# Turning k to tokens with an ordinary product instead of a full transpose, in an HGRN2 and bilinear-FFN kernel

## The chip, the cores and the metric

The kernel runs on one core of one Trainium2 chip. The metric is the device time of one execution in microseconds (us), the median of several runs; lower is better. Five engines work side by side in a core: TensorE (PE; its weight loads are listed as PEld), VectorE (DVE), ScalarE (ACT), GpSimd (POOL) and SyncE (SP, which issues transfers). TensorE writes only to PSUM, and another engine copies from there to SBUF.

## The reference: what is computed

A gated linear recurrence feeds a bilinear feed-forward layer. There are 4 batches, 8 heads, 768 tokens and 48 channels a head; then 3072 tokens of width 384 go through two matrices of 384 by 1536 and one of 1536 by 384. All data of the recurrence is float32.

```python
f = 1.0 / (1.0 + np.exp(-f_logit))
for t in range(S):
    state = f[:, :, t, :, None] * state + np.einsum('bhd,bhe->bhde', k[:, :, t], v[:, :, t])
    y[:, :, t] = np.einsum('bhd,bhde->bhe', q[:, :, t], state)
...
x = attn_out.transpose(0, 2, 1, 3).reshape(B * S, H * D)
a = x @ w_a
b = x @ w_b
return a * b @ w_out
```

The product `k[:, :, t]` by `v[:, :, t]` sums over tokens. TensorE sums over the partition axis, so k, which is loaded with its channels on the partitions, has to be turned until its tokens lie there.

## The kernel before

The recurrence is worked off in 16 units. A unit is one batch, one half of the tokens (384) and four heads: two heads lie one above the other on the partitions (rows 0 to 47 and 64 to 111; rows 48 to 63 and 112 to 127 hold zeros for k), and two such pairs lie side by side (`n` = 0, 1). The tokens of a unit are cut into three chunks (`c`) of 128, and each of these into two of 64 (`p`). For each unit the kernel scales q and k by cumulated products of f (`front`), forms the scores inside 64 tokens (`scores`), turns k (`turn`), sums up the states (`gains`), and forms the output from the scores and the states (`within`, `across`). The constants are D = 48, R = 64, SUB = 64, C = 128, NC = 3, BLK = 384.

```python
def turn(u, spare=False):
    kf = halves(sets[u % NSET]["k"])
    kT = sb1.tile([128, 2, NC, 128], FP32, tag="kT", name="kT")
    ps = pair(spare)
    for n in range(2):
        for c in range(NC):
            o = n * BLK + c * C
            nc.tensor.transpose(ps[n][:, c * C:c * C + C], kf[:, o:o + C], ident)      # L347
        if spare:
            nc.scalar.copy(kT[:, n].rearrange("s c x -> s (c x)"), ps[n][:, 0:BLK])    # L349
    if not spare:
        nc.scalar.copy(kT.rearrange("s n c x -> s n (c x)"), ps_x[:, :, 0:BLK])        # L351
    live[u]["kT"] = kT
    give_back(ps)

def gains(u):
    ...
    for n in range(2):
        for c in range(NC):
            for p in range(2):
                ...
                for h in range(2):
                    r = slice(SUB * p, SUB * p + SUB)
                    nc.tensor.matmul(                                                  # L367
                        ps_x[R * h:R * h + D, p, (n * NC + c) * D:(n * NC + c) * D + D],
                        lhsT=kT[r, n, c, R * h:R * h + D],
                        rhs=t["v"][r, n, c, h * D:h * D + D], start=True, stop=True)
    ...
```

A unit's turning is six transposes, each with a piece of k of 128 channels by 128 tokens as the loaded weights and the 128-column identity as the streamed operand. The first four units use spare PSUM banks (`spare`) and two copies of 384 columns each; the other twelve use `ps_x` and one copy of 768 columns. `gains` writes `ps_x` too, after the copy has read it. In the twelve later units the steps are laid between pieces of the feed-forward layer (its products are L469 in `up`, L542 in `up_pair`, L610 in `down`):

```python
def slot(u):
    nxt = front(u + 1) if u + 1 < NU else iter(())
    next(nxt, None)
    yield
    if u > 2 * NQ:
        within(u - 1)          # L401
    if u < NU:
        scores(u)              # L319
    next(nxt, None)
    yield
    if u < NU:
        turn(u)                # L347, L351
    if u > 2 * NQ:
        across(u - 1)          # L422, and the copies of L435
    yield
    if u < NU:
        gains(u)               # L367
    yield
    ...
```

At each `yield` a piece of the feed-forward layer may follow, of a dozen or more products, or none, as a table of times (`when`, `begun_early`) sets it.

Of the kernel before, what the change touches and what calls it, by code (L numbers as in the profile page):

```python
# [11 lines left out]
FP32 = mybir.dt.float32  # L12
# [7 lines left out]
C = 128  # L20
FINE = (0, 1, 2, 4, 8, 16)
BLK = 384
# [3 lines left out]
R = 64  # L26
# [52 lines left out]
def by_quotients(ctx, tc, q, k, f_logit, v, moe_w_a, moe_w_b, moe_w_out, out, ident, weights, bad):  # L79
    nc = tc.nc  # L80
    B, H, D, S = q.shape
# [5 lines left out]
    NC = BLK // C  # L87
# [9 lines left out]
    sb1 = ctx.enter_context(tc.tile_pool(name="sb1", bufs=1))  # L97
# [32 lines left out]
    def unit(u):  # L130
        b, r = divmod(u, NH * NQ)
        return (b, *divmod(r, NQ))
# [118 lines left out]
    def halves(x):  # L251
        return x.rearrange("p n s -> p (n s)")
# [36 lines left out]
    ps_x, ps_y = (ps_a.tile([128, 2, 512], FP32, tag=n, name=n) for n in ("ps_x", "ps_y"))  # L289
# [14 lines left out]
    def pair(spare=False):  # L304

        return [ps_f[idle.pop(0)] if spare else ps_x[:, i] for i in range(2)]

    def give_back(ps):
        idle.extend(i for x in ps for i, bank in enumerate(ps_f) if bank is x)
# [29 lines left out]
    def turn(u, spare=False):  # L339

        kf = halves(sets[u % NSET]["k"])
        kT = sb1.tile([128, 2, NC, 128], FP32, tag="kT", name="kT")
        ps = pair(spare)
        for n in range(2):
            for c in range(NC):
                o = n * BLK + c * C
                nc.tensor.transpose(ps[n][:, c * C:c * C + C], kf[:, o:o + C], ident)  # L347
            if spare:
                nc.scalar.copy(kT[:, n].rearrange("s c x -> s (c x)"), ps[n][:, 0:BLK])  # L349
        if not spare:  # L350
            nc.scalar.copy(kT.rearrange("s n c x -> s n (c x)"), ps_x[:, :, 0:BLK])  # L351
        live[u]["kT"] = kT
        give_back(ps)

    def gains(u):

        _, half, _ = unit(u)
        t, kT = sets[u % NSET], live[u]["kT"]
        last = half == NH - 1
# [3 lines that stand above are left out]
                    if last and c == NC - 1 and p == 1:  # L363
                        continue
                    for h in range(2):
                        r = slice(SUB * p, SUB * p + SUB)
                        nc.tensor.matmul(  # L367
                            ps_x[R * h:R * h + D, p, (n * NC + c) * D:(n * NC + c) * D + D],
                            lhsT=kT[r, n, c, R * h:R * h + D],
                            rhs=t["v"][r, n, c, h * D:h * D + D],  # L370
                            start=True,
                            stop=True,
                        )
        st = sb3.tile([128, NJ, 2, D], FP32, tag="st", name="st")
        before = live[u - NQ]["st"][NJ] if half else None
        live[u]["st"] = [before] + [st[:, j] for j in range(NJ - 1 if last else NJ)]
        for j in range(NJ - 1 if last else NJ):
            c, p = divmod(j, 2)
            new = ps_x[:, p, 0:2 * NC * D].rearrange("r (n c d) -> r n c d", n=2, c=NC)[:, :, c]
            if before is None:  # L380
                nc.vector.tensor_copy(st[:, j], new)
            else:
                nc.vector.tensor_tensor(st[:, j], before, new, ALU.add)
            before = st[:, j]
        before = live[u]["st"][-1]
        if not last:

            for n in range(2):
                end = products_of_f[u][:, n, BLK - 1:BLK]
                nc.vector.tensor_scalar(before[:, n], before[:, n], end, math.exp(-MIDDLE), ALU.mult, ALU.mult)  # L390
# [261 lines left out]
# [12 lines that stand above are left out]
            turn(u)  # L664
        if u > 2 * NQ:
            across(u - 1)
# [8 lines that stand above are left out]
# [26 lines left out]
    with tc.manual_schedule():  # L701
# [35 lines left out]
        load_unit(2, "v")  # L737
        next(fronts[1])
        turn(0, True)
        within(0)  # L740
        gains(0)
        load_unit(NSET, "f")
        load_weights()
        next(fronts[2])
        turn(1, True)
        across(0)
        load_weights()
        scores(1, True)
        end(2)
        within(1, True)  # L750
        load_unit(2, "q")
        gains(1)
        across(1)
        load_weights()
# [496 lines left out]
```

## Time and profile before

| What | Value |
|---|---|
| Time, median of 3 runs | 630.34 us (629.26 to 631.24) |
| Span of the profiled run | 628.2 us |
| PE busy | 592.5 us (94%), 5922 products |
| PEld busy | 535.6 us (85%), 5922 weight loads |
| DVE busy | 378.2 us (60%) |
| ACT busy | 221.3 us (35%) |
| POOL busy | 63.0 us (10%) |

The profile's page gives the busy time of each engine, the span in 40 slices, the DMA queues, the chain of work that ended last, and the costliest groups of instructions. A group's line has the source line, the engine, the operation, out<-in by tile names, the shapes and the count; then busy time in us and the mean ns of one; then the idle time of the engine before them and what ended it. The mean of a product includes its way through the array, and the next product starts before it is over, so what a stream of products costs is read from the distance between starts. The timeline lists merged pieces: start in us, length in us, engine, line, operation, tiles, shapes, count, and in brackets the idle time before and what ended it.

### The profile page before, as it was taken

The page shows a single profiled execution, that of the slowest core. Times are in us where ns is not written, and L with a number is a line of the kernel's source. Part 1 is how long each engine was busy: PE and PEld are TensorE (multiplying, and loading weights), DVE is VectorE, ACT ScalarE, POOL GpSimd, SP SyncE. Part 2 cuts the span into 40 slices and gives each one's busy share as a digit, 9 for nine tenths or more (in the row PEclk, how much of TensorE's full clock was granted, in tenths as well). Part 3 has the DMA queues.
Part 4 walks back from the last instruction along what each step waited for, and adds up shares of the span by engine and source line. Part 5 has one row for each costly group of instructions (what it writes and reads, how often), then busy time and mean ns, then how long its engine had stood idle before and what let it go on. Part 6 is the DMA issues. An engine that isn't in the chain of part 4 may idle for free.

```text
span 628.2 us, 13968 instructions
## 1 busy us (share of the span) xinstructions
PE 592.5 (94%) x5922; PEld 535.6 (85%) x5922; DVE 378.2 (60%) x748; ACT 221.3 (35%) x400; POOL 63.0 (10%) x58
## 2 busy tenths in 40 slices
PE   0859899999999999999999999999999999999995
PEld 0626555558998999999999999999999999999995
DVE  6868444797887567646675567647564344534541
ACT  6576498822332243224312242323311232022200
POOL 6243154410000000000000000000000000000000
PEclk9959999999999999999999999999999999999999
DMA  8786785000144404130404012040001000000000
GB/s 237 230 255 175 168 263 197 1 1 1 41 109 114 100 3 94 33 91 1 96 1 120 27 36 62 12 110 2 20 1 46 26 20 2 2 27 0 1 26 30
DMA packets 30343, 43.65 MB, mean 69 GB/s; under 512 B 3776, under 2 KB 24896, under 8 KB 30272
## 3 DMA queue, kind: packets, MB, share of 16 engines
q1 hardware_dynamic: 29984, 42.38, 25.0%
q8 instruction: 48, 0.79, 0.5%
q10 hardware_dynamic: 288, 0.30, 0.2%
q14 instruction: 23, 0.19, 0.1%
HBM read 33.23 MB, written 4.72 MB: 60 GB/s over the span
## 4 chain that ended last, share of the span: by engine, by line
PE 88%; DMA 4%; DVE 2%; ACT 2%; SPq 2%; issue 1%; ACTq 0%; DVEq 0%
PE ps_f L542 41%; PE ps_f L610 23%; PE ps_f L469 14%; DMA xT<-y 2%; PE ps_y L401 2%; PE ps_y L422 2%; PE ps_x L319 2%; PE ps_x L367 2%; PE ps_x L347 1%; SPq L154 1%; DMA raw<-in_moe_w_b_dram 1%; SPq L450 1%; DMA out_dram<-o 1%; ACT y L435 1%; DVE h L605 0%
## 5 line engine op out<-in xcount | busy, mean ns | idle before, releaser
L542 PE MATMUL ps_f<-xT,w_ba 128*128 128x192 f32 x864 | 155.4, 327 | 0.0
L547 DVE TENSOR_TENSOR groups<-ps_f,groups 128x384 f32<-128x384 f32 x144 | 80.1, 557 | 118.5 <-ACT groups L559 99.3
L542 PEld LDWEIGHTS ps_f<-xT,w_ba 128*128 128x128 f32 x864 | 142.3, 190 | 0.5
L469 PE MATMUL ps_f<-xT,w_ba 128*128 128x384 f32 x288 | 98.4, 502 | 7.9 <-DVE w_ba L216 5.9
L469 PEld LDWEIGHTS ps_f<-xT,w_ba 128*128 128x128 f32 x288 | 55.3, 195 | 47.8 <-DVE w_ba L216 7.0
L542 PE MATMUL ps_f<-b_sb,raw 128*128 128x192 f32 x432 | 82.0, 326 | 0.0
L542 PEld LDWEIGHTS ps_f<-b_sb,raw 128*128 128x128 f32 x432 | 72.2, 190 | 0.0
L550 ACT COPY groups<-ps_f 128x384 f32<-128x384 f32 x36 | 17.2, 478 | 109.3 <-PE ps_f L542 103.5
L610 PE MATMUL ps_f<-w_out,h 128*128 128x192 f32 x288 | 52.0, 330 | 0.3 <-DVE o L605 0.3
L610 PE MATMUL ps_f<-w_out,groups 128*128 128x192 f32 x288 | 50.9, 327 | 0.0
L610 PE MATMUL ps_f<-spare,h 128*128 128x192 f32 x288 | 49.6, 328 | 0.2 <-DVE h L605 0.2
L610 PEld LDWEIGHTS ps_f<-w_out,h 128*128 128x128 f32 x288 | 46.8, 190 | 1.3 <-DVE o L605 0.6
L610 PEld LDWEIGHTS ps_f<-w_out,groups 128*128 128x128 f32 x288 | 47.3, 190 | 0.1
L610 PEld LDWEIGHTS ps_f<-spare,h 128*128 128x128 f32 x288 | 46.7, 190 | 0.8 <-issue 0.5
L205 POOL TENSOR_SCALAR h<-h 128x768 f32<-128x768 f32 (+1 forms) x20 | 40.7, 2037 | 50.8 <-ACT h L202 50.8
L266 POOL TENSOR_SCALAR inv<-inv 128x768 f32<-128x768 f32 x14 | 13.5, 962 | 305.7 <-ACT inv L262 305.7
L605 DVE TENSOR_TENSOR o<-ps_f,u 128x192 f32<-128x192 f32 x36 | 12.8, 356 | 43.7 <-PE ps_f L610 40.8
L572 DVE TENSOR_TENSOR groups<-groups 128x384 f32<-128x384 f32 x72 | 36.6, 550 | 0.0
L559 ACT COPY groups<-ps_f 128x384 f32<-128x384 f32 x36 | 17.2, 478 | 52.7 <-PE ps_f L542 52.7
L542 PE MATMUL ps_f<-xT,raw 128*128 128x192 f32 x144 | 29.8, 330 | 0.0
L542 PE MATMUL ps_f<-b_sb,w_ba 128*128 128x192 f32 x144 | 29.3, 326 | 0.0
L319 PE MATMUL ps_x<-q_in,k_in 48*64 48x64 f32 x672 | 13.7, 226 | 16.2 <-DMA raw<-in_moe_w_b_dram 15.4
(113 smaller groups left out, 697.4 us busy)
## 6 DMA issues: line engine op xcount, KB each, us to landing
q_in<-in_q_dram SPq DMA_DIRECT2D x32, 144.0 KB, 4.0
k_in<-in_k_dram SPq DMA_DIRECT2D x32, 144.0 KB, 3.5
v_in<-in_v_dram SPq DMA_DIRECT2D x16, 288.0 KB, 5.1
raw<-in_moe_w_out_dram SPq DMA_DIRECT2D x6, 768.0 KB, 4.3
out_dram<-o SPq DMA_DIRECT2D x24, 192.0 KB, 1.9
f_in<-in_f_logit_dram SPq DMA_DIRECT2D x28, 144.0 KB, 3.0
xT<-y SPq DMA_DIRECT2D x46, 72.0 KB, 2.2
raw<-in_moe_w_b_dram SPq DMA_DIRECT2D x4, 768.0 KB, 7.2
```

The costliest lines, as they stand in the source:

```text
L205: nc.gpsimd.tensor_scalar(h, h, HI_MAX, None, ALU.min)
L266: nc.gpsimd.tensor_scalar(inv, inv, EXP_K, 1.0, ALU.mult, ALU.add)
L319: nc.tensor.matmul(ps[h][SUB * p:SUB * p + SUB, o:o + SUB], lhsT=kf[r, tokens(n, c, p)], rhs=qf[r, tokens(n, c, p)], start=True, stop=True,)
L367: nc.tensor.matmul(ps_x[R * h:R * h + D, p, (n * NC + c) * D:(n * NC + c) * D + D], lhsT=kT[r, n, c, R * h:R * h + D], rhs=t["v"][r, n, c, ...
L469: nc.tensor.matmul(ps[nm][:, 0:BLK], lhsT=w[:, kt, ft * 128:ft * 128 + 128], rhs=x[:, kt], start=kt == 0, stop=kt == NKT - 1,)
L542: nc.tensor.matmul(to[:, g], lhsT=w[:, g, j], rhs=x, start=start and g == 0, stop=True, skip_group_check=True)
L547: nc.vector.tensor_tensor(c[:, :, k, i], x, y, ALU.add)
L550: nc.scalar.copy(p1, x0)
L559: nc.scalar.copy(u3, x0)
L572: nc.vector.tensor_tensor(to[:, :, 2 * j + k], a[:, :, k], b[:, :, k], ALU.mult)
L605: nc.vector.tensor_tensor(to, x, y, op)
L610: nc.tensor.matmul(to, lhsT=x[:, i], rhs=w[:, i], start=first and i == 0, stop=i == HFT - 1, skip_group_check=True)
```

## The change

The transpose is replaced by an ordinary matrix product with the same weights (the piece of k), whose streamed operand is not the whole identity but its columns 0 to 47 and 64 to 111, those of channels that exist. The turned k then has 96 columns a chunk instead of 128, the copies from PSUM shrink with it, and the weights of `gains` are read at 48 h instead of 64 h. It is meant to leave out the empty columns, in the stream and in the copy.

```diff
         kf = halves(sets[u % NSET]["k"])
-        kT = sb1.tile([128, 2, NC, 128], FP32, tag="kT", name="kT")
+        kT = sb1.tile([128, 2, NC, 2 * D], FP32, tag="kT", name="kT")
+        heads = ident.rearrange("p (h r) -> p h r", h=2)[:, :, 0:D]
         ps = pair(spare)
         for n in range(2):
             for c in range(NC):
                 o = n * BLK + c * C
-                nc.tensor.transpose(ps[n][:, c * C:c * C + C], kf[:, o:o + C], ident)
+                to = ps[n][:, 2 * D * c:2 * D * c + 2 * D].rearrange("s (h d) -> s h d", h=2)
+                nc.tensor.matmul(to, lhsT=kf[:, o:o + C], rhs=heads, start=True, stop=True)
             if spare:
-                nc.scalar.copy(kT[:, n].rearrange("s c x -> s (c x)"), ps[n][:, 0:BLK])
+                nc.scalar.copy(kT[:, n].rearrange("s c x -> s (c x)"), ps[n][:, 0:NC * 2 * D])
         if not spare:
-            nc.scalar.copy(kT.rearrange("s n c x -> s n (c x)"), ps_x[:, :, 0:BLK])
+            nc.scalar.copy(kT.rearrange("s n c x -> s n (c x)"), ps_x[:, :, 0:NC * 2 * D])
...
-                            lhsT=kT[r, n, c, R * h:R * h + D],
+                            lhsT=kT[r, n, c, D * h:D * h + D],
```

## The prediction

> **What bounds the kernel now.** I read the busy table and the 40 slices first, then the idle time of TensorE by what ended it, then the groups of the lines concerned, and last the timeline around single turns.
>
> ```profile
> PE 592.5 (94%) x5922; PEld 535.6 (85%) x5922; DVE 378.2 (60%) x748; ACT 221.3 (35%) x400; POOL 63.0 (10%) x58
> PE   0859899999999999999999999999999999999995
> PEclk9959999999999999999999999999999999999999
> ```
>
> TensorE is the bound from the fourth slice on. Before that it waits: the list of waits gives it 15.4 us for the first data and 5.9 us for converted weights. After 66 us the same list holds only five waits of TensorE, 3.0 us in all. So a nanosecond taken from TensorE's stream after about 70 us counts in full; one taken before mostly turns into waiting for weights, and ScalarE's time counts only where TensorE waits for its copy.
>
> From the costliest groups with shapes kept apart, the turn, its copy and two rows to compare with:
>
> ```profile
> L347 PE MATMUL ps_x<-ident,k_in 128*128 128x128 f32 x72 | 9.8, 273 | 0.0
> L347 PEld LDWEIGHTS ps_x<-ident,k_in 128*128 128x128 f32 x72 | 8.6, 141 | 0.3
> L610 PE MATMUL ps_f<-w_out,h 128*128 128x192 f32 x288 | 52.0, 330 | 0.3 <-DVE o L605 0.3
> L610 PEld LDWEIGHTS ps_f<-w_out,h 128*128 128x128 f32 x288 | 46.8, 190 | 1.3 <-DVE o L605 0.6
> L351 ACT COPY kT<-ps_x 128x768 f32<-128x768 f32 x12 | 9.6, 800 | 16.1 <-PE ps_x L347 16.1
> ```
>
> The second and fourth rows are the important pair. Both load 128 columns of float32 weights, but the transpose's load takes 141 ns and the ordinary product's 190 ns.
>
> One turn of the steady part in the timeline:
>
> ```profile
> 199.11 0.49 PE L610 MATMUL ps_f<-w_out,h 128*128 128x192 f32 x2
> 199.28 0.74 PEld L347 LDWEIGHTS ps_x<-ident,k_in 128*128 128x128 f32 x6
> 199.44 0.82 PE L347 MATMUL ps_x<-ident,k_in 128*128 128x128 f32 x6
> 200.18 0.74 PEld L422 LDWEIGHTS ps_y<-q_in,st 48*48 48x48 f32 x48 [0.17 <-issue]
> 200.19 0.89 PE L422 MATMUL ps_y<-q_in,st 48*48 48x64 f32 x48
> 200.29 0.80 ACT L351 COPY kT<-ps_x 128x768 f32<-128x768 f32 x1 [1.73 <-PE ps_x L347]
> 201.14 0.35 PEld L367 LDWEIGHTS ps_x<-v_in,kT 64*48 64x48 f32 x22 [0.22 <-ACT kT L351]
> 201.15 0.47 PE L367 MATMUL ps_x<-v_in,kT 64*48 64x48 f32 x20
> ```
>
> Six transposes take 0.82 us from the first start to the last end, one lasts 0.273: five distances in 0.547, so **109 ns from start to start**. The last one starts at 199.44 + 0.547 = 199.99, and the small products of L422 start 0.20 later. The copy ends at 201.09, and L367, the gains, starts at 201.15: here TensorE waits for the copy. The whole chain of work that ended last, between 140 and 240 us, names the copy in just three places (about 0.81 us each, at 185.29, 200.29 and 232.48). In the other nine slots a feed-forward piece lies between, and the gains start 1.0 to 4.0 us after the copy's end.
>
> **What the Trainium skill says.** (1) "TensorE: Matmul & The Clock Gate", section "LDWEIGHTS (loading the stationary operand)", gives columns / 1.2 ns: 107 ns for 128 columns. The trace agrees for ordinary products: at 152.97 us, where a feed-forward piece starts with nothing ahead of it, the second load starts 108 ns after the first. It does not for the transposes' loads, which are 49 ns shorter in the record. (2) "FP8 and Floating Point Precision" lists true FP32 as four passes through the array. The trace has two clocks a column: the 192-column products of L610 start 163 ns apart, 192 x 2 / 2.4 = 160 and a few ns more. (3) "TensorEngine Tiling (Array Packing)", "Key Properties", says that a change of tiling mode drains TensorE. The trace agrees: after the last transpose the small L422 products come 0.20 us later, a full-size product 0.11 us later (turn at 149.59 us). (4) "Perfetto Trace Analysis", "Transposes", advises a transpose for a logical transpose and not a standard product. No run here shows yet what that is worth in float32.
>
> **The change part by part.**
>
> *Instructions.* 96 transposes (72 in the late slots, 24 in the first four units) become 96 ordinary products, at the same places in TensorE's order, with the same waits. The 20 copies shrink by a quarter. Nothing is added or moved.
>
> *The stream.* A transpose streams 128 columns: 128 x 2 / 2.4 = 107 ns, plus 2 is the 109 measured. The new product streams 96: 80 + 2 = 82 ns. But its load is now an ordinary one. Take the part of a load's 190 ns that the array can't share: 107 ns by the measured 108 above. (The transpose's, by 141 against 190, is some 58 ns and hides behind 107 of streaming.) Weights of the next product load while this one streams, in the trace each load starts as the product before it starts; so the distance is the longer of the two: max(82, 107 + 2) = **109 ns**. The limit passes from the stream to the load and nothing is won: 96 x 0 = 0. The first new load hides behind a 192-column product of 163 ns, as before. In the two early turns at half clock (213 ns apart) both sides double alike.
>
> *The drain.* The last product of a turn needs no load after it of its own kind. Where the small L422 products follow, in 11 of the 12 late slots, their start comes with the end of the drain. One 96-column product lasts about 273 - 32 x 0.85 = 246 ns (the slope is from 218 ns for 64 columns, 273 for 128 and 327 for 192). So L422 starts 27 ns earlier. In eight slots that is all: 8 x 27 = 0.22 us. In the slot where L610 follows, its own 107 ns load sets the distance: 0.
>
> *The copy.* It goes from 768 to 576 columns. 798 ns for 768 columns and 478 for 384 make 0.833 ns a column: 192 x 0.833 = 160 ns less, 638 in place of 798. On the path in three slots, with the 27 ns of the drain ahead of it: the copy ends 187 ns earlier. Could L367 start so early? Before, it starts 70 to 84 ns after the modelled end of the last L422 product, whereas streams that wait for nothing start some 200 ns ahead of that end; so there are over 250 ns to take, and the copy remains what ends the wait. 3 x 187 = 0.56 us.
>
> *The first 70 us.* Of the eight 384-column copies, each 80 ns shorter, one stands in the way, at 51.5 us (gains wait for the first half): 80 + 27 = 0.11 us. The turns around 17, 22 and 63 us have a mask product of DVE or small products between copy and use. I count 0.11 us, knowing that a wait for weights may take it.
>
> Sum: 0 + 0.22 + 0.56 + 0.11 = 0.89 us, 0.14%: 630.34 - 0.89 = **629.5 us**.
>
> **The rivals.** *The stream sets the pace.* If the ordinary load were hidden as the transpose's is, the distance falls from 109 to 82 ns: 84 warm products x 27 = 2.3 us, of which 11 x 27 = 0.3 are counted already, so some 627.5 us. For it: the load's pace alone is seen just once or so, since everywhere else 160 ns of streaming cover it. Against: 190 ns recorded against 141. I give it one in ten.
> *The ordinary product is dearer.* The skill's advice (4), four passes (2), or slow reading of the identity's two separate groups of 48 columns: at four passes 96 x (160 - 109) = 4.9 us more, some 634. If loads and products did not overlap, 107 + 82 = 189 ns apart, 96 x 80 = 7.7 us more, some 637. Against it: L610 streams ordinary float32 products at two clocks a column with loads fully hidden. That separate groups cost something no row rules out; a few ns each would cancel the gain (96 x 9 ns = 0.9 us). One in ten in all, mostly for the few ns.
> *The won wait comes back.* At 196 us TensorE waits 0.7 us for DVE's scaled k, so what two slots win before it could be lost there: 0.37 us at most, 629.8. Against: that DVE work itself starts when TensorE ends a product at 189.06, which would come earlier too.
>
> **Range and chances.** The mechanisms leave 627.5 to 631.3. The three runs of before lie 2 us apart, more than my whole gain, so that scatter sets the width: 628.2 to 630.9 should hold it 8 times in 10. Two per cent is 12.6 us; no rival gets there. Faster by over 2%: 0.01; within 2%: 0.98; slower by over 2%: 0.01.
>
> **What would show it.** In the changed profile: the loads of the turn (there L349) at about 190 ns, not 141; its products at about 246 ns, started 109 ns apart, not 82; the small products of `across` (there L424) 175 ns after the last of them; copies of 638 and 398 ns; gains at the three slots still released by the copy, 0.19 us earlier after their turn. It would be wrong if the six products started clearly closer than 109 ns (the load is not the limit) or farther apart (separate groups or load and stream in turn), or if PE's sum of waits after 70 us changed by more than 0.5 us.

## The result, and the profile after

The changed kernel takes 638.62 us (638.45 to 639.82) against 630.59 us (629.26 to 631.24) for the kernel before: **1.34% slower, ratio 1.0134, interval 1.0113 to 1.0155** (the two medians alone lie 8.0 us, 1.27%, apart). Predicted were 629.5 us, 628.2 to 630.9.

The busy line of the page after:

```profile
PE 603.9 (95%) x6018; PEld 548.5 (86%) x6018; DVE 377.9 (59%) x748; ACT 219.0 (34%) x400; POOL 62.2 (10%) x58
```

The count is what to look at: 6018 products and 6018 loads, where there were 5922. That is 96 more of each, and 96 is exactly the number of transposes replaced. TensorE's busy time is up by 11.4 us and that of its weight loads by 12.9; no other engine changes by more than 2.3 us.

The groups that answer to the turn, its copy and the ordinary product shown before:

```profile
L349 PE MATMUL ps_x<-ident,k_in 128*128 128x96 f32 x144 | 17.7, 273 | 0.0
L349 PEld LDWEIGHTS ps_x<-ident,k_in 128*128 128x128 f32 x144 | 17.6, 192 | 0.0
L353 ACT COPY kT<-ps_x 128x576 f32<-128x576 f32 x12 | 7.7, 639 | 24.0 <-PE ps_x L349 24.0
```

The late units have 72 products in the source; the record has 144. The load is the 190 ns kind, as foreseen, and the copy is 639 ns, as foreseen, but the copy's engine now waits longer for TensorE, 24.0 us over the twelve copies in place of 16.1.

The same turn as before, in the timeline after:

```profile
203.81 1.47 PEld L349 LDWEIGHTS ps_x<-ident,k_in 128*128 128x128 f32 x12
203.97 1.47 PE L349 MATMUL ps_x<-ident,k_in 128*128 128x96 f32 x12
...
205.37 0.89 PE L424 MATMUL ps_y<-q_in,st 48*48 48x64 f32 x48
205.48 0.64 ACT L353 COPY kT<-ps_x 128x576 f32<-128x576 f32 x1 [2.38 <-PE ps_x L349]
206.17 0.35 PEld L369 LDWEIGHTS ps_x<-v_in,kT 64*48 64x48 f32 x21
206.17 0.47 PE L369 MATMUL ps_x<-v_in,kT 64*48 64x48 f32 x19
```

Twelve loads and twelve products, where six of each stood. From the first start to the last it is 1.20 us (1.47 less 0.27), where it was 0.55. From the start of the small products (205.37) to that of the gains (206.17) it is 0.80 us, where it was 0.96: the shorter copy does bring its 0.16 us. From the first late turn to the end the two traces have 638.1 - 152.27 = 485.8 us and 628.2 - 149.59 = 478.6 us. The two traces differ by 9.9 us (the profiled run was the slowest of the changed kernel's four): **7.2 us arise from the first late turn on**, 2.7 before it. What those 2.7 are is taken up under e7_early.

The ratio could have been read off before the change. These are groups of the kernel before:

```profile
L319 PE MATMUL ps_x<-q_in,k_in 48*64 48x64 f32 x672 | 13.7, 226 | 16.2 <-DMA raw<-in_moe_w_b_dram 15.4
L319 PE MATMUL ps_f<-q_in,k_in 48*64 48x64 f32 x96 | 2.2, 238 | 0.0
L347 PE MATMUL ps_x<-ident,k_in 128*128 128x128 f32 x72 | 9.8, 273 | 0.0
L347 PE MATMUL ps_f<-ident,k_in 128*128 128x128 f32 x24 | 4.4, 333 | 0.0
```

`scores` (L319) issues 24 products a unit, 384 in 16 units; the record has 672 + 96 = 768. `turn` issues 6 transposes a unit, 96; the record has 72 + 24 = 96. So an ordinary float32 product runs here as two pairs of load and product, a float32 transpose as one.

### The profile page after: what moved, and what is told of

Its sections match the earlier page's. It is cut to its first block, busy times and chain, and to the rows that moved or that the text cites. A ratio compares the mean times of both kernels' runs of the same rounds, so it can differ in the third digit from the quotient of the medians.

```text
span 638.1 us, 14160 instructions
## 1 busy us (share of the span) xinstructions
PE 603.9 (95%) x6018; PEld 548.5 (86%) x6018; DVE 377.9 (59%) x748; ACT 219.0 (34%) x400; POOL 62.2 (10%) x58
## 3 DMA queue, kind: packets, MB, share of 16 engines
q1 hardware_dynamic: 29984, 42.38, 24.5%
## 4 chain that ended last, share of the span: by engine, by line
PE 90%; DVE 4%; DMA 3%; ACT 1%; SPq 1%; issue 1%; ACTq 0%; DVEq 0%
PE ps_f L544 41%; PE ps_f L612 24%; PE ps_f L471 14%; PE ps_x L349 2%; DMA xT<-y 2%; PE ps_y L424 2%; PE ps_y L403 2%; PE ps_x L319 2%; PE ps_x L369 2%; PE ps_f L349 1%; DVE inv L281 1%; DMA out_dram<-o 1%; DVE groups L271 1%; DMA f_in<-in_f_logit_dram 1%; DVE h L607 0%
## 5 line engine op out<-in xcount | busy, mean ns | idle before, releaser
L319 PE MATMUL ps_x<-q_in,k_in 48*64 48x64 f32 x672 | 13.7, 227 | 16.3 <-DVE start L276 15.6
```

The lines of the kernel that those rows point to most:

```text
L319: nc.tensor.matmul(ps[h][SUB * p:SUB * p + SUB, o:o + SUB], lhsT=kf[r, tokens(n, c, p)], rhs=qf[r, tokens(n, c, p)], start=True, stop=True,)
```

## The experiments

The theory after the result: **two pairs in place of one** for each turned piece, at about the same time a pair, and nothing else of weight. The rivals: the streamed operand in two groups of 48 columns, or the compact layout, is slow (then the whole identity would be harmless); the extra work hides and the loss arises in the first 150 us; the stream, not the load, sets the pace. The runs of before beside these have a median of 630.23 us.

### e1_copy: the short copy alone

```diff
-            nc.scalar.copy(kT.rearrange("s n c x -> s n (c x)"), ps_x[:, :, 0:BLK])
+            nc.scalar.copy(kT.rearrange("s n c (h d) -> s n (c h) d", h=2),
+                ps_x[:, :, 0:BLK].rearrange("s n (ch r) -> s n ch r", r=R)[:, :, :, 0:D])
...
-                            lhsT=kT[r, n, c, R * h:R * h + D],
+                            lhsT=kT[r, n, c, D * h:D * h + D],
```

The transposes stay; the copies of the first four units are shortened in the same way.

> The transposes of before stay (one pass over 128 columns), only the copy takes the 96 existing columns out of PSUM (pieces of 48 with a step of 64) and the gains read their weights at 48 h. Theory (an ordinary float32 product runs as two loads and two products, a transpose as one; that alone is the loss): 5922 products, starts in a turn 109 ns apart, copies of about 640 ns instead of 798, three slots start their gains 0.16 us earlier; 0.3 to 0.8 us faster than before, ratio 0.9987 to 0.9996. Rival (the compact layout costs: pieces of 48 in the copy or weights at 48 h are slow): a copy longer than 798 ns or longer gains, and a time at or above before.

Measured: 630.12 us, ratio 0.9992 (0.9983 to 1.0001). Its copy and the gains behind it, groups and timeline:

```profile
L354 ACT COPY kT<-ps_x 128x576 f32<-128x576 f32 x12 | 7.7, 639 | 16.1 <-PE ps_x L347 16.1
```

```profile
200.46 0.89 PE L428 MATMUL ps_y<-q_in,st 48*48 48x64 f32 x48
200.57 0.64 ACT L354 COPY kT<-ps_x 128x576 f32<-128x576 f32 x1 [1.73 <-PE ps_x L347]
...
201.26 0.52 PE L373 MATMUL ps_x<-v_in,kT 64*48 64x48 f32 x26
```

The copy that reads pieces of 48 with a step of 64 is as short as the one that reads them in a row (639 ns), and the gains start 0.80 us after the small products, as in the changed kernel. So the compact layout costs nothing that shows. The 0.5 us of three slots is at the edge of what the runs resolve: the interval holds both it and no gain at all. In the trace the late part is 478.4 us against 478.6, with one wait of TensorE at L616, 0.8 us, that is 0.5 us longer than its like before; the DVE work ahead of it waited 3.3 us for an output transfer instead of 2.8.

### e2_full: the ordinary product with the whole identity

```diff
-                nc.tensor.transpose(ps[n][:, c * C:c * C + C], kf[:, o:o + C], ident)
+                nc.tensor.matmul(ps[n][:, c * C:c * C + C], lhsT=kf[:, o:o + C], rhs=ident, start=True, stop=True)
```

> Only the transpose becomes an ordinary product with the whole identity of 128 columns in one run; layout and copies stay as before. Theory of two passes: 6018 products, twelve starts a turn 111 to 112 ns apart, since the load of 128 columns and not the stream of 128 or 96 is the limit; slots longer by about 0.67 us, 9 us over before (8 to 11), a little over the changed kernel because the copies are not shorter. Rival (the operand of two separate groups of 48 is what is slow): 5922 products or no longer turns, time within 1 us of before.

Measured: 639.33 us, ratio 1.0152 (1.0136 to 1.0168). The groups:

```profile
L347 PE MATMUL ps_x<-ident,k_in 128*128 128x128 f32 x144 | 18.0, 275 | 0.0
L347 PEld LDWEIGHTS ps_x<-ident,k_in 128*128 128x128 f32 x144 | 17.6, 192 | 0.0
```

Again 144 for 72, with one group of 128 columns. The starts lie 109 to 112 ns apart, a late turn is 1.226 us from first to last start; 12 x (1.226 - 0.546) = 8.2 us, and the part from the first late turn to the end is 486.7 us, 8.1 more than before. The two groups of 48 are not the cause; the ordinary product of two pairs is.

### e3_twice: each transpose issued twice

```diff
-                nc.tensor.transpose(ps[n][:, c * C:c * C + C], kf[:, o:o + C], ident)
+                for _ in range(2):
+                    nc.tensor.transpose(ps[n][:, c * C:c * C + C], kf[:, o:o + C], ident)
```

> Each transpose is issued twice into the same place; nothing else is changed, the second leaves the same values. Theory of two passes: what counts is the number of load-and-product pairs, so twelve starts a turn 109 ns apart, 6018 products and 8 to 11 us over before, as with the ordinary product, within 1 us of the kernel with the whole identity. Rival (the extra pairs are hidden in waits and the loss of the changed kernel comes from elsewhere, the start or the later waits): under 3 us over before.

Measured: 638.70 us, ratio 1.0137 (1.0122 to 1.0152).

```profile
L348 PE MATMUL ps_x<-ident,k_in 128*128 128x128 f32 x144 | 17.7, 273 | 0.0
L348 PEld LDWEIGHTS ps_x<-ident,k_in 128*128 128x128 f32 x144 | 16.5, 141 | 0.3
```

All starts are 109 or 110 ns apart. A kernel with the cheap loads, but with twice as many pairs, loses the same 8 us as the changed one. So the number of pairs explains the loss, and it is paid in full: 12 x (1.201 - 0.546) = 7.9 us worked out, 7.7 us in the trace's late part.

### e5_bf16: the ordinary product in one pass

```diff
-                nc.tensor.matmul(to, lhsT=kf[:, o:o + C], rhs=heads, start=True, stop=True)
+                words, ones_ = (x.bitcast(BF16).rearrange("p (n two) -> p n two", two=2)[:, :, 1] for x in (kf[:, o:o + C], ident))
+                nc.tensor.matmul(to, lhsT=words, rhs=ones_.rearrange("p (h r) -> p h r", h=2)[:, :, 0:D], start=True, stop=True)
```

This is the changed kernel with the upper halves of the words as bf16. The turned k loses the lower 16 bits of each word, so it isn't a version of the same kernel.

> The changed kernel, but the product takes the upper halves of k's words and of the identity's as bf16, so the turned k is cut to bf16 (part of its precision is left out); same 96 columns in two groups, same copies. Theory of two passes: bf16 runs in one pass, 5922 products, with a load no longer than the transpose's; starts 50 to 70 ns apart, so a turn 0.25 to 0.35 us shorter than before; 3 to 5 us faster than before, about 626. Rival (an ordinary product or its two separate groups cost more as such): starts over 109 ns apart or more pairs, and a time over 630.

Measured: 624.66 us, ratio 0.9920 (0.9904 to 0.9935).

```profile
L350 PE MATMUL ps_x<-ident,k_in 128*128 128x96 bf16 x72 | 5.1, 206 | 0.0
```

```profile
197.32 0.44 PEld L350 LDWEIGHTS <-k_in 128*128 128x128 bf16 x6
197.48 0.43 PE L350 MATMUL ps_x<-ident,k_in 128*128 128x96 bf16 x6
197.84 0.74 PEld L427 LDWEIGHTS ps_y<-q_in,st 48*48 48x48 f32 x48
```

An ordinary product with the same two groups of 48, but 72 for 72, and 42 to 47 ns apart, closer than the 50 to 70 expected. A late turn is 0.22 us from first to last start, 0.32 less than with transposes, as expected, and the small products follow its last product after 134 ns instead of 203. The gain is 5.6 us by the medians and 5.0 by the ratio, at or above the upper end of 3 to 5. Of this the late part of the trace accounts for 4.3 us (474.3 against 478.6). The rest lies before it, where the four early turns are 2.0 us shorter in sum and TensorE was granted the full clock, against 0.95 of it in the trace of before (first 145 us); how much each brought is not separated here. So an ordinary product as such need not cost more than a transpose. In float32 it does, and there it has two pairs.

### e6_late and e7_early: where the loss is paid

The product only in the twelve late units (e6), or only in the first four (e7); the other units keep the transposes, with the short copy of 96 columns.

```diff
+                if spare:          # e6_late; e7_early has: if not spare
+                    nc.tensor.transpose(ps[n][:, c * C:c * C + C], kf[:, o:o + C], ident)
+                    continue
                 to = ps[n][:, 2 * D * c:2 * D * c + 2 * D].rearrange("s (h d) -> s h d", h=2)
```

> The product with 96 columns only in the twelve late units; the first four keep the transposes (with the short copy of 96 columns). Theory: 72 more pairs, 5994 products; each late turn 1.20 us from first to last start instead of 0.55, 12 x 0.654 = 7.8 us, less 3 x 0.16 for the copies, no loss before the first late turn: 7.0 to 7.8 us over before, about 637.6. Rival (most of the loss arises in the first 150 us, where the changed kernel's profile is 2.7 us late at its first late turn): under 6 us over before.

> The product with 96 columns only in the first four units; the twelve late ones keep the transposes (with the short copy of 96 columns). Theory: 24 more pairs, 5946 products; TensorE has 3.7 us more work there, but waits for weights and transfers in that stretch take most of it up: 0.3 to 1.5 us over before, about 631. Rival (the first stretch has no room): 2.5 to 3.7 us over before, about 633.5.

Measured: e6_late 636.61 us, ratio 1.0105 (1.0091 to 1.0119); e7_early 630.33 us, ratio 1.0003 (0.9989 to 1.0016). Their busy lines, e6_late first:

```profile
PE 600.1 (95%) x5994; PEld 544.8 (86%) x5994; DVE 377.7 (59%) x748; ACT 218.9 (34%) x400; POOL 62.4 (10%) x58
```

```profile
PE 596.0 (95%) x5946; PEld 539.7 (86%) x5946; DVE 378.0 (60%) x748; ACT 219.1 (35%) x400; POOL 62.1 (10%) x58
```

72 and 24 more pairs. The late ones cost 6.4 us in the median (5.7 to 7.5), somewhat under what I expected, and 7.0 us by the late part of the trace (485.7 against 478.6). The early ones cost nothing that can be measured (0.1 us, -0.7 to 1.0), a little less than I expected, although their four turns are 3.2 us longer in sum. The two runs together make 6.5 us, where the changed kernel lost 8.0; the intervals allow that difference.

The waits before 150 us show where the early turns' time went. Before, e7_early and e6_late in this order, TensorE's largest wait that the early turns can shorten:

```profile
PE ps_f L469 <- DVE w_ba L216: 5.9, 1, 5.9
PE ps_f L477 <- DVE w_ba L216: 3.7, 1, 3.7
PE ps_f L477 <- DVE w_ba L216: 3.5, 1, 3.5
```

The feed-forward products wait for converted weights. This one wait does not prove the point, since it is as short in e6_late, whose early turns are the short ones. The sum does: of the first 145 us TensorE is idle for 27.3 to 28.0 in the three traces whose early turns are transposes issued once (before, e1_copy, e6_late), and for 24.5 to 26.9 in the five whose early turns have twice as many float32 pairs. So a longer early turn is at least in part taken out of waits. That the changed kernel's profiled run reached its first late turn 2.7 us late is mostly scatter: e7_early and e8_onehead have the same turns in that stretch, and reached it at 150.1 and 150.8 us instead of 152.3.

### e8_onehead: half the stream

```diff
+                if not spare:
+                    nc.tensor.matmul(to[:, 0], lhsT=kf[:, o:o + C], rhs=heads[:, 0], start=True, stop=True)
+                    continue
```

The changed kernel, but the late units stream 48 columns and leave the second head's k out.

> The changed kernel, but in the twelve late units each product streams only the 48 columns of the first head; the second head's k is not turned (left out), the copy still takes 96 columns. Theory (the load of 128 float32 columns, not the stream, sets the pace): still twelve starts a turn about 112 ns apart, time within 0.8 us of the changed kernel, about 638.2. Rival (the stream sets it): starts about 42 ns apart, turns 0.7 us shorter, time about 631 or less.

Measured: 637.69 us, ratio 1.0124 (1.0109 to 1.0139).

```profile
L350 PEld LDWEIGHTS ps_x<-ident,k_in 128*128 128x128 f32 x144 | 17.6, 192 | 0.0
L350 PE MATMUL ps_x<-ident,k_in 128*128 128x48 f32 x144 | 17.2, 269 | 0.0
```

```profile
202.29 1.47 PEld L350 LDWEIGHTS ps_x<-ident,k_in 128*128 128x128 f32 x12
202.45 1.43 PE L350 MATMUL ps_x<-ident,k_in 128*128 128x48 f32 x12
```

Half the columns, the same loads in the same 1.47 us. The time is 0.9 us under the changed kernel's, where I had allowed 0.8; the shorter first distance makes 12 x 0.04 = 0.5 of it. Only the first distance, whose load has been hidden behind feed-forward work, follows the stream: 43 ns here, 83 with 96 columns, 109 with 128. The others are 111 to 112 ns with 48, 96 and 128 columns alike (110 to 113 in the changed kernel's own trace). So the stream does not set the pace. That the load of 128 float32 columns does is the likely reading, since the loads follow one another without a gap; it is inferred, as no run loads fewer columns.

## Why the prediction was wrong

**The step that failed** stands under "Instructions": "96 transposes become 96 ordinary products ... Nothing is added". They became 192 pairs. Everything that the sum calls "The stream" was multiplied by the wrong number: not 6 x 109 ns before and 6 x 109 after, but 6 x 109 and 12 x 111. The twelve late turns pay 12 x (1.200 - 0.546) = 7.85 us, where the term said 0. Less 3 x 0.16 for the copies that makes 7.4; the trace has 7.2 there, the runs 8.0 in all (7.1 to 9.8 by the interval). e3_twice, which changes only the number of pairs, and e5_bf16, whose product has one pair (and a shorter one), show it from both sides. None of the prediction's signs of being wrong names a count, and none of them came clearly: the starts are 111 to 112 ns apart, and TensorE's waits after 70 us hardly changed. The counts of the kernel before held the answer.

**How the error came in** is in the second place of the skill. "FP8 and Floating Point Precision", section "TensorE Precision Notes", has four passes for true FP32; I set against it that the 192-column products start 163 ns apart, two clocks a column, and took the page to be refuted. The pace itself was read rightly: 384-column products (L469) start 323 ns apart, so 192 more columns cost 160 ns. But 163 ns is the distance of two records, and a source product has two. It is 326 ns a product of the source, by the same reckoning four clocks a column: this agrees with the page, and the transpose, with one record at two clocks a column, takes half of that. The advice in "Perfetto Trace Analysis", "Transposes", holds here too: with the identity whole in both, the transpose saves 9.1 us (e2_full). I named that rival ("four passes", some 634) but in the stream alone, 51 ns a product; in the late turns it is 223 - 109 = 114. The other rival, some 637, comes nearest to the measured 638.6, but by chance: it had loads and products taking turns, 189 ns apart, and that did not happen. The range of "627.5 to 631.3" left both of these out, at one chance in ten together.

**The pace of a pair was right.** 109 was predicted, 111 to 112 came, and the stream no longer sets it (e2_full, e8_onehead), as "The stream" says. That the load does in its place fits, but is inferred. That a quarter less in the stream brings nothing holds.

**The drain was wrong, and small.** The small products start 204 to 205 ns after the last product of the turn, as after a transpose (203), not 175. The 0.22 us of that term did not come, nor the 27 ns of it in each copy slot. The record shows where the sum went wrong: it took a product of 96 columns to last 246 ns, which holds for the first of a turn alone. The later ones last 275 ns with 48, 96 and 128 columns alike (e8_onehead, the changed kernel, e2_full), and the small products come 205 ns after the last in all three. Why the later ones last longer was not tried.

**The copy was right.** 639 and 398 ns against 638 and 398; the gains start 0.16 us earlier in each of the three slots, as the copy's term has it without the drain's share. It could not outweigh the pairs, and by itself (e1_copy) it can't be told from nothing. No version here that computes the same is clearly faster than the kernel before.

**The first 70 us** were right in kind: what is added there costs nothing that can be measured, since TensorE waits less (e7_early). The 0.11 us counted there is below what the runs resolve.

## What to carry to other kernels

Compare the count of a line in the profile with the count in the source before reckoning with a mean duration: where a product of one kind has two records and the operation it replaces has one, the cost doubles before any size plays a part. For float32 data of this size, turn with the transpose and not with an ordinary product. Narrowing what is streamed brings nothing where the stream does not set the pace, as with these loads of 128 float32 columns; look for that limit first.

## What was not expected of the hardware

- In a row of them, a float32 transpose of 128 by 128 takes 109 ns of TensorE, an ordinary float32 product with 128 loaded columns 223 ns, with 48, 96 or 128 columns streamed alike.
- With 128 loaded and 96 streamed columns, ordinary bf16 products start 42 to 47 ns apart, one to a source product; in float32 the starts are 111 to 112 ns apart, two to a source product. So the float32 product takes five times as long, 223 against about 44 ns.
- In a run of ordinary float32 products whose starts are 111 to 112 ns apart, the record gives each but the first 275 ns, whether 48, 96 or 128 columns are streamed; the first takes 206, 246 and 273 ns.
- A copy of ScalarE from PSUM in pieces of 48 with a step of 64 takes 639 ns for 576 columns, the same as for columns in a row.
